# Attention on Trainium2: transposes and projections on 64x128 tiles, four double PSUM banks, loads by tensor, another order

## The chip, the core and the metric

The kernel runs on one NeuronCore of one Trainium2 chip. A core has five engines with queues of their own: PE (TensorE, matrix multiplies out of SBUF into PSUM), DVE (VectorE), ACT (ScalarE), POOL (GpSimd) and SP (SyncE, which here issues the transfers between HBM and SBUF). They meet only through semaphores. PSUM has eight banks. The metric is device time in microseconds (us) of one execution. Most executions of one kernel agree within 0.3%.

## What is computed

A linear attention over q, k, v of shape (8, 8, 576, 64) and then a mixture of eight experts on its result. The attention, per batch and head:

```python
def phi(x):
    proj = np.einsum('bhsd,df->bhsf', x, w_phi)                     # 64 -> 128
    proj = proj - np.max(np.abs(proj), axis=-1, keepdims=True)
    return np.concatenate([np.exp(proj), np.exp(-proj)], axis=-1)   # 256 features
q_p, k_p = (phi(q), phi(k))
kv = np.einsum('bhsf,bhsd->bhfd', k_p, v)
z = np.sum(k_p, axis=2)
num = np.einsum('bhsf,bhfd->bhsd', q_p, kv)
den = np.einsum('bhsf,bhf->bhs', q_p, z)[..., None] + 1e-06
return num / den
```

The expert stage takes the 4608 rows of 512, forms logits with `w_gate`, assigns rows to experts greedily by logit (576 rows to each), and runs `relu(x @ w1[e]) @ w2[e]`. All arithmetic here is float32 or finer splits of it.

## The kernel before

**Units.** Attention works in 16 units: a pair of batches times a pair of heads. Per unit `load` (line 105) brings q, k and v as tiles `qi`, `ki`, `vi` of 128 partitions x 2 x 9 x 64; `ki` and `vi` come in four transfers each, `qi` in two.

**Steps of a unit**, by the names that the plan uses. `kt` (line 165): nine 128x128 transposes of k on PE in three groups, copied to SBUF by ACT as `kh`. `kg` (line 152): the projection by `w_phi`, in three blocks of 12 matmuls on 64x64 tiles of the array, into a double bank. DVE then takes the maximum (`km`, line 156) and subtracts it (`ks`, line 159, tile `kt`), ACT takes both exponentials (lines 177, 178, tile `kP`). `kv` (lines 189, 194): k features times v, on 128x64 tiles and a last piece on 64x64. POOL sums the features (`ad`, lines 201 to 205). `bd` (line 222) and `z` (line 234) bring the sums and the gate weights into `kz`. For q: `qt` (line 243), `qg` (line 152), `qm` and `qs` on DVE, then `T` (line 255), 18 more 128x128 transposes, and the exponentials on ACT (line 258, tile `qP`). Last `num` (line 279): the numerators, denominators and logits on 128x64 tiles, in four pieces a unit, and for each the division on DVE (lines 283 to 298).

**PSUM.** Two single banks S0, S1 (transposes of q and k, z, num, counts), two double banks D0, D1 (projections, bd, T) and two single banks for kv.

**Order.** No loop order is written out. `Plan` (line 17) gets every step with its engine, a duration, a due time, its dependencies and the buffers that it takes and frees, and lists the steps; the program is then issued in that list's order, so each engine runs its queue strictly in it. Due times come from the table `ATT`. The plan also places pieces of the expert stage's preparation (`init`: tables made by POOL and DVE, lines 360 to 424) into the attention.

**After attention** comes the routing of the first expert (DVE and PE in turns, from line 433 on), then the expert stage.

Of the kernel before, what the change touches and what calls it, by code (L numbers as in the profile page):

```python
# [17 lines left out]
class Plan:  # L18
# [3 lines left out]
    SEM=40.; dl=0.; wp=6.  # L22
# [5 lines left out]
    def order(self):  # L28
# [7 lines left out]
        while left:  # L36
            best=None; horizon={}
            cand={}
            for x in left:
# [9 lines left out]
                if not ok: continue  # L49
                for kind,n,u in x['slot']:  # L50
                    h=held.setdefault(kind,[0.]*n)
                    z=[t for t in h if t is not None]
                    if not z: ok=False; break
                    r=max(r,min(z)+self.SEM)
# [35 lines left out]
def attention(ctx, tc, nc, q, k, v, w_phi, w_gate, xs, L, C, xp, cfg={}, after=None, later=None, count=None, init=iter(())):  # L90
# [3 lines left out]
    d=dict(TI=21.,kt=-4.,kg=0.,kv=4.,bd=4.,z=5.,zc=6.,qt=6.,qg=10.,T=2.5,num=26.,stay=2.,ks=4.,qs=4.,ns=5.,ng=6,ld=60.,nqP=8,init=25.,pitch=1.)  # L94
# [7 lines left out]
    p=ps.tile([128,512],F32,name='S0',bufs=1)  # L102
    for _ in range(cfg.get('nwarm',7)): PE.matmul(p,w[:,0:128],w,start=True,stop=True)
    T={}
    HS=S*D
    def load(u,first=lambda: None):
        bp,hp=divmod(u,NP)
        qi=sb.tile([128,2,9,D],F32,name='qi',bufs=2); ki=sb.tile([128,2,9,D],F32,name='ki',bufs=2); vi=sb.tile([128,2,9,D],F32,name='vi',bufs=3)
        T['q',u],T['k',u],T['v',u]=qi,ki,vi
        def put(t,p,s0,s1,x,b,row):  # L110
# [23 lines left out]
    dv=lambda n,ps_=True: (150 if ps_ else 110)+1.03*n-95  # L134
    ac=lambda n,ps_=True: (170 if ps_ else 200)+.83*n-100
    QI=227.
    def unit(u):
        bp,hp=divmod(u,NP)
        t0=u*d['TI']
        def add(name,eng,dur,due,fn,deps=(),mode=None,slot=(),frees=(),lat=None,after=0.):  # L140
            P.add((name,u),eng,dur,t0+due,fn,[(x,u) for x in deps],
                  lat={'PE':170.,'DVE':95.,'ACT':100.,'POOL':30.,'SP':0.}[eng] if lat is None else lat,mode=mode,slot=slot,frees=frees,after=after)
        add('ld','SP',600. if u else 0.,-d['ld'],lambda x: load(u) if u else None,slot=(('qi',2,('qi',u)),('ki',2,('ki',u)),('vi',3,('vi',u))),lat=4500. if u else 0.)
        def slots(*l): return tuple((kd,n,(kd,u) if len(z)==0 else (kd,u)+tuple(z)) for kd,n,*z in l)
        ld0=('ld',)

        def project(x,X,src,i0,i1):
            p=X['p']=bank(X['b'],[128,2,512])(x)
            for i in range(i0,i1):
                for c in range(2):  # L150
                    for r in range(2):
                        PE.matmul(p[64*(c^r):64*(c^r)+64,r,128*(i-i0):128*(i-i0)+128],src[64*r:64*r+64,i,64*(c^r):64*(c^r)+64],C['w'][64*r:64*r+64,:],start=True,stop=True,skip_group_check=True)  # L152
# [8 lines left out]
        for g in range(3):  # L161
            def pe(x,g=g):
                if g==0: T['kh',u]=sb.tile([128,9,128],F32,name='kh',bufs=2)
                p=T['ktp',u,g]=bank(('S',u,'kt',g),[128,3,128])(x)
                for i in range(3): PE.transpose(p[:,i],ch(T['k',u],3*g+i),ident)  # L165
            def act(x,g=g): A.copy(T['kh',u][:,3*g:3*g+3],T['ktp',u,g])
            due=d['kt']+d['ks']*1.5*g
            add(('kt',g),'PE',327.,due,pe,ld0,'A',slots(('S',NS,'kt',g),*((('kh',2),) if g==0 else ())),(('ki',u),),after=(5500.,9000.,10000.)[g] if u==0 else 0.)
            add(('kh',g),'ACT',ac(384),due+.4,act,(('kt',g),),frees=(('S',u,'kt',g),))
        for g in range(3):  # L170
# [8 lines left out]
            add(('kg',g),'PE',3*QI,due,pe,[('kh',g)],'Q',slots(('D',ND_,'kg',g)),(('kh',u),),after=8000. if u==0 else 0.)  # L179
            add(('km',g),'DVE',dv(768),due+.8,lambda x,X=X: maxima(X,'km',3),(('kg',g),))  # L180
            add(('ks',g),'DVE',dv(768),due+1.4,lambda x,X=X: differ(X,'kt',3),(('km',g),),slot=slots(('ktt',3,g)),frees=(('D',u,'kg',g),))
            add(('ke',g),'ACT',2*ac(768,False),due+2.,act,(('ks',g),),slot=slots(('kP',2)) if g==0 else (),frees=(('ktt',u,g),))
        for g in range(2):
            def pe(x,g=g):
                kP=T['kP',u]; v_=T['v',u]
                if g==0: T['kvps',u]=[ps.tile([128,256],F32,name='kv%d'%i,bufs=1) for i in range(2)]
                for i,b in KV[g]:
                    a,s_=divmod(b,9); c=a^i
                    PE.matmul(T['kvps',u][i][64*c:64*c+64,:],v_[:,a,s_,:],kP[:,b,:],start=b in (0,5,9,14),stop=False,skip_group_check=True)  # L189
                if g==1:  # L190
# [19 lines left out]
        def kvt(x):  # L210
            kt=T['kvT',u]=sb.tile([128,2,256],F32,name='kvT',bufs=2)
            for i in range(2): A.copy(kt[:,i],T['kvps',u][i])
# [677 lines left out]
```

## Time and profile before

| | us |
|---|---|
| median of 3 runs (857.32 to 858.21) | 858.2 |
| the profiled execution | 857.9 |
| its span, first to last instruction | 856.1 |
| PE busy in the span | 803.4 |
| DVE busy | 570.2 |
| ACT busy | 370.0 |
| POOL busy | 262.1 |

The profile is one execution. A row of a timeline gives the start from the span's start, the length, engine, source line, operation, tiles (written <- read), shape and count; in brackets stands how long the engine had been idle ahead of it and what ended the wait. A float32 matmul shows as two records on PE, a transpose as one. The shape of a PE row begins with the tile of the array, rows*columns. Ends of matmuls are modelled, so prices on PE are best read from one block's start to the next. PEld are the loads of the stationary operand, which run beside the matmuls. A row of stretches gives, after start, end and length, the busy time of each engine with the number of its instructions, then the granted PE clock, the share of the DMA engines and GB/s.

### The profile page before, as it was taken

The page shows a single profiled execution, that of the slowest core. Times are in us where ns is not written, and L with a number is a line of the kernel's source. Part 1 is how long each engine was busy: PE and PEld are TensorE (multiplying, and loading weights), DVE is VectorE, ACT ScalarE, POOL GpSimd, SP SyncE. Part 2 cuts the span into 40 slices and gives each one's busy share as a digit, 9 for nine tenths or more (in the row PEclk, how much of TensorE's full clock was granted, in tenths as well). Part 3 has the DMA queues.
Part 4 walks back from the last instruction along what each step waited for, and adds up shares of the span by engine and source line. Part 5 has one row for each costly group of instructions (what it writes and reads, how often), then busy time and mean ns, then how long its engine had stood idle before and what let it go on. Part 6 is the DMA issues. An engine that isn't in the chain of part 4 may idle for free.

```text
span 856.1 us, 24776 instructions
## 1 busy us (share of the span) xinstructions
PE 803.4 (94%) x10508; PEld 685.8 (80%) x10508; DVE 570.2 (67%) x1534; ACT 370.0 (43%) x691; POOL 262.1 (31%) x300
## 2 busy tenths in 40 slices
PE   4879999999999999758999999999999999999995
PEld 2768887887788878658979879889889798898984
DVE  1787788778867887577858658668667577461410
ACT  1646665566566565413334324333333243251410
POOL 1654455555555555111040130310301202401001
PEclk9999999999999999958999999999999999999999
DMA  8424444454445421134143340532233225610301
GB/s 170 116 54 113 114 114 126 118 135 121 117 120 134 117 58 31 57 114 131 54 147 118 129 147 35 177 131 95 97 118 123 83 104 185 214 63 38 118 13 43
DMA packets 73534, 91.88 MB, mean 107 GB/s; under 512 B 5280, under 2 KB 56512, under 8 KB 73424
## 3 DMA queue, kind: packets, MB, share of 16 engines
q1 hardware_dynamic: 67328, 71.32, 29.3%
q0 software_dynamic: 6096, 18.98, 6.5%
q8 instruction: 83, 1.36, 0.7%
q14 instruction: 27, 0.22, 0.1%
HBM read 71.40 MB, written 18.87 MB: 105 GB/s over the span
## 4 chain that ended last, share of the span: by engine, by line
PE 69%; issue 16%; DVE 7%; POOL 4%; DMA 2%; ACT 1%; SPq 0%; POOLq 0%; DVEq 0%; ACTq 0%
PE h L763 19%; PE y L792 16%; PE S L279 7%; PE D L152 6%; PE kv L189 4%; PE D L255 3%; PE y L807 2%; PE S L165 2%; PE S L243 2%; PE h L739 2%; PE S L234 2%; DVE km L156 1%; PE rps L530 1%; POOL out_dram L821 1%; DVE kt L159 1%
## 5 line engine op out<-in xcount | busy, mean ns | idle before, releaser
L763 PE MATMUL h<-xh,w1h 128*128 128x272 f32 (+1 forms) x512 | 145.9, 305 | 0.7 <-ACT xh L740 0.7
L763 PE MATMUL h<-xh,w1l 128*128 128x304 f32 (+1 forms) x512 | 143.9, 301 | 0.0
L774 ACT ACTIVATE fh<-h 128x272 fp32r<-128x272 f32 (+1 forms) x128 | 49.2, 384 | 134.5 <-PE h L763 122.1
L821 POOL DMA_INDIRECT out_dram<-ysb,idx x40 | 40.5, 1012 | 207.0 <-ACT ysb L815 203.5
L792 PE MATMUL y<-w2h,fl 128*128 128x512 f32 x256 | 102.0, 398 | 0.0
L792 PE MATMUL y<-w2l,fh 128*128 128x512 f32 x256 | 101.9, 398 | 0.0
L792 PE MATMUL y<-w2h,fh 128*128 128x512 f32 x256 | 101.5, 396 | 0.0
L763 PEld LDWEIGHTS h<-xh,w1h 128*128 128x128 f32 x512 | 97.2, 190 | 2.5 <-issue 1.2
L763 PEld LDWEIGHTS h<-xh,w1l 128*128 128x128 f32 x512 | 97.4, 190 | 0.0
L734 POOL DMA_INDIRECT xg<-xs,idx x40 | 40.0, 1000 | 178.2 <-issue 141.5
L763 PE MATMUL h<-xl,w1h 128*128 128x272 f32 (+1 forms) x512 | 91.4, 298 | 0.0
L778 DVE SCALAR_TENSOR_TENSOR fl<-h,fh 128x272 fp32r<-128x272 f32 (+1 forms) x128 | 52.8, 419 | 55.6 <-ACT fh L774 41.9
L201 POOL TENSOR_TENSOR ks<-kP 128x512 f32<-128x512 f32 x32 | 40.9, 1277 | 157.1 <-issue 130.2
L279 PE MATMUL S<-kz,qP 128*64 128x73 f32 x2304 | 87.4, 230 | 1.0 <-ACT xp L296 1.0
L279 PEld LDWEIGHTS S<-kz,qP 128*64 128x64 f32 x2304 | 78.1, 137 | 11.0 <-issue 9.1
L202 POOL TENSOR_TENSOR ks<-ks,kP 128x512 f32<-128x512 f32 x64 | 81.5, 1273 | 4.9
L258 ACT ACTIVATE qP<-D 128x768 f32<-128x768 f32 x96 | 72.5, 808 | 9.1 <-PE D L255 5.6
L763 PEld LDWEIGHTS h<-xl,w1h 128*128 128x128 f32 x512 | 75.5, 188 | 0.0
L815 ACT COPY ysb<-y 128x512 f32<-128x512 f32 (+1 forms) x40 | 21.8, 544 | 104.4 <-PE y L792 72.3
L156 DVE TENSOR_REDUCE km<-D 128x6 f32<-128x768 f32 x48 | 45.7, 953 | 29.4 <-PE D L152 29.2
L189 PE MATMUL kv<-kP,vi 128*64 128x256 f32 x512 | 60.9, 379 | 0.0
L156 DVE TENSOR_REDUCE qm<-D 128x6 f32<-128x768 f32 x48 | 45.6, 950 | 20.0 <-PE D L152 19.8
(177 smaller groups left out, 1550.5 us busy)
## 6 DMA issues: line engine op xcount, KB each, us to landing
raww<-in_moe_w_dram SPq DMA_DIRECT2D x64, 512.0 KB, 5.5
qi<-in_q_dram SPq DMA_DIRECT2D x32, 288.0 KB, 4.6
xs<-xp SPq DMA_DIRECT2D x16, 576.0 KB, 3.8
ki<-in_k_dram SPq DMA_DIRECT2D x32, 160.0 KB, 3.8
vi<-in_v_dram SPq DMA_DIRECT2D x32, 160.0 KB, 5.2
ki<-in_k_dram SPq DMA_DIRECT2D x32, 128.0 KB, 3.7
vi<-in_v_dram SPq DMA_DIRECT2D x32, 128.0 KB, 5.0
xg<-xs,idx POOLq DMA_INDIRECT x40, 3.5
```

The costliest lines, as they stand in the source:

```text
L152: PE.matmul(p[64*(c^r):64*(c^r)+64,r,128*(i-i0):128*(i-i0)+128],src[64*r:64*r+64,i,64*(c^r):64*(c^r)+64],C['w'][64*r:64*r+64,:],start=True ...
L156: V.tensor_reduce(m[:,:,0:n],X['v'],axis=AX.X,op=OP.max,apply_absolute_value=True)
L189: PE.matmul(T['kvps',u][i][64*c:64*c+64,:],v_[:,a,s_,:],kP[:,b,:],start=b in (0,5,9,14),stop=False,skip_group_check=True)
L201: if i==0: G.tensor_add(ks[:,:,a],X(0),X(1))
L202: elif i<3: G.tensor_add(ks[:,:,a],ks[:,:,a],X(i+1))
L258: for fh in range(2): A.activation(qP[:,fh].rearrange('p (b i) f -> p b (i f)',b=2),X['T'][:,:,0:384],AF.Exp,scale=1.0-2*fh)
L279: PE.matmul(p[64*ab:64*ab+64,j-j0,:],T['qP',u,jj][:,fh,o,64*ab:64*ab+64],T['kz',u][:,ab,fh,a^ab,:],start=fh==0,stop=fh==1)
L763: PE.matmul(p,ws[:,k,o:o+128],xx[:,k,o1:o2],start=n==0,stop=n==11)
L774: A.activation(hh[:,f,o1:o1+m1],p[:,0:m1],AF.Relu)
L778: V.scalar_tensor_tensor(hl[:,f,o1:o1+m1],p[:,0:m1],0.0,hh[:,f,o1:o1+m1],op0=OP.max,op1=OP.subtract)
L792: PE.matmul(p,hx[:,f,o:o+128],ws[:,f%2,:],start=n==0,stop=n==23)
L821: st=G.indirect_dma_start(out=ov,out_offset=bass.IndirectOffsetOnAxis(ap=iv,axis=0),in_=yv,in_offset=None)
```

## The change

*Tiles.* A 128x128 transpose becomes a pair of transposes on 64x128 tiles (`turn`): one for partitions 0 to 63, one for 64 to 127, each into its own bank of a double bank. A projection block becomes six matmuls on 64x128 tiles instead of twelve on 64x64. kv, z and num stay on 128x64, bd and kv's last piece on 64x64. The transposes of q and k come in two groups (3 and 6 of the nine) instead of three, and ACT's copies with them.

*Banks.* All PSUM tiles of attention come from four double banks D0 to D3. num and its division come in two pieces a unit instead of four; the last unit's scaling is done by DVE and no longer by ACT.

*Loads* of k, q and v are steps of their own, each with its own due time and its own wait for a free buffer.

*Order.* `ATT` gets an `off` table with a due time for each step, and tables `o0` and `oL` for the first and the last unit; the plan's costs change (`swc`, `swA`, `swO`, `wp`, `QI`, `QT`, `dv`, `ac`). A step may now ask for several buffers of one kind.

```diff
@@ load
-    def load(u,first=lambda: None):
-        bp,hp=divmod(u,NP)
-        qi=sb.tile([128,2,9,D],F32,name='qi',bufs=2); ki=sb.tile([128,2,9,D],F32,name='ki',bufs=2); vi=sb.tile([128,2,9,D],F32,name='vi',bufs=3)
+    def load(u,n,first=lambda: None):
+        bp,hp=divmod(u,NP); b=2*bp
+        x=dict(q=q,k=k,v=v)[n]
+        t=T[n,u]=sb.tile([128,2,9,D],F32,name=n+'i',bufs=3 if n=='v' else 2)
...
-    P=Plan(d['stay']*1e3)
-    ND_,NS=2,2
-    def bank(u_,shape):
-        return lambda x: ps.tile(shape,F32,name='%s%d'%(u_[0],x['buf'][u_]),bufs=1)
+    P=Plan(d['stay']*1e3); P.swc,P.swA,P.swO,P.wp=90.,85.,35.,d['wp']
+    ND_=4
+    def bank(u_):
+        return lambda x: ps.tile([128,2,512],F32,name='D%d'%x['buf'][u_],bufs=1)
+    def turn(p,n,f):
+        for i in range(n):
+            for r in range(2): PE.transpose(p[:,r,64*i:64*i+64],f(i)[64*r:64*r+64,:],ident[64*r:64*r+64,64*r:64*r+64])
+    halves=lambda p,n: p[:,:,0:64*n].rearrange('p r (i t) -> p r i t',t=64)
+    rows=lambda t: t.rearrange('p i (r t) -> p r i t',r=2)
...
+    BK=((0,3),(3,9))
...
-    QI=227.
+    QI,QT=239.,61.
...
-        add('ld','SP',600. if u else 0.,-d['ld'],lambda x: load(u) if u else None,slot=(('qi',2,('qi',u)),('ki',2,('ki',u)),('vi',3,('vi',u))),lat=4500. if u else 0.)
+        for n,nb in (('k',2),('q',2),('v',3)):
+            def f(x,n=n): load(u,n,(lambda: C.update(weights(ctx,tc,nc,w_gate,C))) if u==0 and n=='k' else lambda: None)
+            add(('ld',n),'SP',2950.,-d['ld']+(0. if n=='k' else .1 if n=='q' else .2),f,slot=slots((n+'i',nb)),lat=2200. if u or n!='k' else 3400.)
...
             for i in range(i0,i1):
-                for c in range(2):
-                    for r in range(2):
-                        PE.matmul(p[64*(c^r):64*(c^r)+64,r,128*(i-i0):128*(i-i0)+128],src[64*r:64*r+64,i,64*(c^r):64*(c^r)+64],C['w'][64*r:64*r+64,:],start=True,stop=True,skip_group_check=True)
+                for r in range(2): PE.matmul(p[:,r,128*(i-i0):128*(i-i0)+128],src[64*r:64*r+64,i,:],C['w'][64*r:64*r+64,:],start=True,stop=True,skip_group_check=True)
...
-                p=X['T']=bank(('D',u,'T',g),[128,2,512])(x)
+                p=X['T']=bank(('D',u,'T',g))(x)
                 t=X['t'].rearrange('p i r f -> p (i r) f')
-                for i in range(6): PE.transpose(p[:,i//3,128*(i%3):128*(i%3)+128],t[:,i],ident)
+                turn(p,6,lambda i: t[:,i])
...
-                    if u==NU-1:
-                        for j in range(n): A.activation(x_[:,j0+j,64*a:64*a+64],p[:,j,0:64],AF.Copy,scale=rd[:,j,:])
-                    else:
-                        V.tensor_mul(x_[:,j0:j1,64*a:64*a+64],p[:,:n,0:64],rd[:,:n].to_broadcast([128,n,64]))
+                for c in range(2): V.tensor_mul(x_[:,5*c:9 if c else 5,64*a:64*a+64],v_[:,c,0:5-c,0:64],rd[:,c,0:5-c].to_broadcast([128,5-c,64]))
...
-ATT = {'TI': 20.56, 'kt': -4.44, 'kg': -1.69, 'kv': 7.48, 'bd': 4.17, 'z': 4.87, 'qt': -1.35, 'qg': 6.68, 'T': 12.67, 'num': 33.16, 'stay': 2.23, 'ks': 2.72, 'qs': 4.94, 'ns': 4.35, 'nqP': 6}
+ATT = {'TI': 21.607, 'kt': -4.44, 'kg': -1.69, 'kv': 7.48, 'bd': 4.17, 'z': 4.87, 'qt': -1.35, 'qg': 6.68, 'T': 12.67, 'num': 33.16, 'stay': 5.079, 'ks': 2.72, 'qs': 4.94, 'ns': 4.35, 'nqP': 6, 'wp': 2929.132, 'off': {('ld', 'k'): -72.48, ('ld', 'q'): -53.32, ('ld', 'v'): -55.81, ('kt', 0): -3.08,
...
```

What the new order does to the queues, at three places. Lines of the new program are a few higher: 130 are the transposes, 158 the projections, 229 bd, 242 z, 285 num.

PE at the start of attention, before; `ki_96` is the first unit's k, `ki_119` the second's:

```order
L165 MATMUL S0_132<-ident_69,ki_96 128x128 x3
L165 MATMUL S1_137<-ident_69,ki_119 128x128 x3
L152 MATMUL D0_143<-w_65,kh_131 64x128 x12
L165 MATMUL S0_158<-ident_69,ki_96 128x128 x3
L243 MATMUL S1_166<-ident_69,qi_95 128x128 x3
```

and in the changed program, where `ki_97` is the first unit's k and `ki_113` the second's:

```order
L130 MATMUL D0_119<-ident_69,ki_97 128x64 x6
L130 MATMUL D1_126<-ident_69,ki_97 128x64 x12
L158 MATMUL D2_141<-w_65,kh_118 128x128 x6
L130 MATMUL D3_149<-ident_69,qi_110 128x64 x6
L158 MATMUL D0_156<-w_65,kh_118 128x128 x6
L158 MATMUL D1_171<-w_65,kh_118 128x128 x6
L158 MATMUL D3_180<-w_65,qh_148 128x128 x6
L130 MATMUL D2_195<-ident_69,ki_113 128x64 x6
```

The second unit's k moved from the second block to behind four projections of the first unit.

PE in a unit in the middle, before (z, a projection, transposes of k, q and T, num, projections):

```order
L234 MATMUL S_2254<-one,ks 64x1 x16
L152 MATMUL D_2275<-w,kh 64x128 x12
L165 MATMUL S_2289<-ident,ki 128x128 x3
L243 MATMUL S_2295<-ident,qi 128x128 x3
L255 MATMUL D_2300<-ident,qtt 128x128 x6
L279 MATMUL S_2310<-kz,qP 64x73 x16
L152 MATMUL D_2330<-w,kh 64x128 x12
```

and changed:

```order
L285 MATMUL D_2893<-kz,qP 64x73 x36
L242 MATMUL D_2937<-one,ks 64x1 x16
L130 MATMUL D_2965<-ident,qi 128x64 x12
L158 MATMUL D_2978<-w,kh 128x128 x6
L158 MATMUL D_2992<-w,qh 128x128 x6
L130 MATMUL D_3001<-ident,qtt 128x64 x12
L285 MATMUL D_3017<-kz,qP 64x73 x36
```

num and z, both on 128x64 tiles, now stand side by side, and the transposes and projections that follow are all on 64x128.

SP's queue behind the first unit's k, before:

```order
L113 DMA qi_95<-in_q_dram 64x2x576 x2
L113 DMA vi_97<-in_v_dram 64x2x320
L113 DMA vi_97<-in_v_dram 64x2x256
L113 DMA vi_97<-in_v_dram 64x2x320
L113 DMA vi_97<-in_v_dram 64x2x256
L113 DMA ki_119<-in_k_dram 64x2x320
L113 DMA ki_119<-in_k_dram 64x2x256
```

and changed:

```order
L114 DMA qi_110<-in_q_dram 64x2x576 x2
L114 DMA ki_113<-in_k_dram 64x2x320
L114 DMA ki_113<-in_k_dram 64x2x256
L114 DMA ki_113<-in_k_dram 64x2x320
L114 DMA ki_113<-in_k_dram 64x2x256
L114 DMA vi_166<-in_v_dram 64x2x320
L114 DMA vi_166<-in_v_dram 64x2x256
```

The second unit's k moved ahead of the first unit's v.

More of the change, by code (lines that the diff above doesn't have):

```diff
@@ L18 @@
 class Plan:
[L22 removed]
+    SEM=40.; dl=0.; wp=6.; swc=95.; swA=100.; swO=50.
     def __init__(self,stay=0.): self.t=[]; self.by={}; self.stay=stay
@@ L49, in order @@
                 if not ok: continue
+                want={}
                 for kind,n,u in x['slot']:
[L51 to L54, printed above, removed]
+                    h=held.setdefault(kind,[0.]*n); i=want[kind]=want.get(kind,-1)+1
+                    z=sorted(t for t in h if t is not None)
+                    if i>=len(z): ok=False; break
+                    r=max(r,z[i]+self.SEM)
                 if not ok: continue
@@ L101, in attention, with put @@
     w=sb.tile([128,512],BF,name='warm',bufs=1); V.memset(w,0.0)
[L102 to L103 removed]
+    p=ps.tile([128,2,512],F32,name='D0',bufs=1)
+    for _ in range(cfg.get('nwarm',7)): PE.matmul(p[:,0],w[:,0:128],w,start=True,stop=True)
     T={}
     HS=S*D
[L106 to L110 removed]
+    def load(u,n,first=lambda: None):
+        bp,hp=divmod(u,NP); b=2*bp
+        x=dict(q=q,k=k,v=v)[n]
+        t=T[n,u]=sb.tile([128,2,9,D],F32,name=n+'i',bufs=3 if n=='v' else 2)
+        def put(p,s0,s1,b,row):
             n=s1-s0
@@ L185, in pe @@
                 kP=T['kP',u]; v_=T['v',u]
-                if g==0: T['kvps',u]=[ps.tile([128,256],F32,name='kv%d'%i,bufs=1) for i in range(2)]
+                if g==0: T['kvps',u]=bank(('D',u,'kv'))(x)
+                kv=T['kvps',u]
                 for i,b in KV[g]:
                     a,s_=divmod(b,9); c=a^i
-                    PE.matmul(T['kvps',u][i][64*c:64*c+64,:],v_[:,a,s_,:],kP[:,b,:],start=b in (0,5,9,14),stop=False,skip_group_check=True)
+                    PE.matmul(kv[64*c:64*c+64,i,0:256],v_[:,a,s_,:],kP[:,b,:],start=b in (0,5,9,14),stop=False,skip_group_check=True)
                 if g==1:
@@ L210, in kvt @@
         def kvt(x):
-            kt=T['kvT',u]=sb.tile([128,2,256],F32,name='kvT',bufs=2)
-            for i in range(2): A.copy(kt[:,i],T['kvps',u][i])
+            T['kvT',u]=sb.tile([128,2,256],F32,name='kvT',bufs=2)
+            A.copy(T['kvT',u],T['kvps',u][:,:,0:256])
         kend=d['kv']+4*d['ks']
-        add(('kvt',),'ACT',2*ac(256),kend+1.,kvt,[('kv',1)],frees=(('kv',u),))
+        add(('kvt',),'ACT',ac(512),kend+1.,kvt,[('kv',1)],frees=(('D',u,'kv'),))
         def bdp(x):
-            p=T['kfp',u]=bank(('D',u,'bd'),[128,2,512])(x)
+            p=T['kfp',u]=bank(('D',u,'bd'))(x)
             for i in range(2):
@@ new lines, in unit, with pe @@
+            h=2*hp+a
+            X={}
+            due=d['num']+d.get('ns',5.1)*2*a
+            def pe(x,a=a,X=X):
+                p=X['p']=bank(('D',u,'num',a))(x)
+                for j in range(9):
+                    jj,o=divmod(9*a+j,6); c,m=divmod(j,5); m*=73
+                    for fh in range(2):
+                        for ab in range(2):
+                            PE.matmul(p[64*ab:64*ab+64,c,m:m+73],T['qP',u,jj][:,fh,o,64*ab:64*ab+64],T['kz',u][:,ab,fh,a^ab,:],start=fh==0,stop=fh==1,skip_group_check=True)
```

154 lines of the change are left out of this document (72 added, 82 removed).

## The prediction

> **What bounds the kernel now.** I read the stretches by stage first, to see which engine is full where.
>
> ```profile
> core 0: us, PE busy (x) PEld busy (x) DVE busy (x) ACT busy (x) POOL busy (x), PEclk, DMA share, GB/s
> 0.00:17.30 17.30, 5.28 (x13) 1.83 (x13) 1.98 (x5) 1.76 (x2) 2.89 (x8) 1.00 0.85 182
> ...
> 40.00:60.00 20.00, 15.46 (x258) 12.40 (x255) 16.98 (x46) 9.41 (x16) 14.22 (x17) 0.91 0.27 61
> 60.70:326.70 266.00, 259.97 (x5599) 216.83 (x5595) 210.98 (x453) 165.65 (x274) 137.44 (x130) 1.00 0.44 112
> 356.10:856.10 500.00, 474.44 (x3626) 415.05 (x3626) 303.55 (x953) 161.08 (x340) 85.02 (x121) 0.97 0.32 107
> ```
>
> Attention fills the first 356 us. In the first 17.3 PE works 5.3, and between 40 and 60 it works 15.5 of 20. From 60.7 to 326.7 (13 units, from one bd block to the bd block 13 units later) PE is busy for 260 of 266 us: a unit takes 20.46 us and PE sets it. DVE has 211 us in there, 16.2 a unit, and would be next. The 500 us behind attention are the expert stage. Its instructions stand in the same order in both programs on every engine from the routing on, so it should only move as a block. Everything the change can do lies in the first 356 us: PE's steady work, the 17.3 us in which PE does almost nothing, the dip at 40 to 60, and the hand-over.
>
> **Prices on PE.** Inside a steady unit the timeline gives them from one block's start to the next.
>
> ```profile
> 199.78 0.82 PE L255 MATMUL D<-ident,qtt 128*128 128x128 f32 x6
> 200.44 0.49 PE L165 MATMUL S<-ident,ki 128*128 128x128 f32 x3
> ...
> 202.99 0.68 PE L222 MATMUL D<-bd,kvT 64*64 64x72 f32 x32
> 203.59 1.10 PE L234 MATMUL S<-one,ks 128*64 128x1 f32 x32
> 204.62 0.89 PE L152 MATMUL D<-w,kh 64*64 64x128 f32 x24
> ...
> 206.15 0.82 PE L255 MATMUL D<-ident,qtt 128*128 128x128 f32 x6
> 206.90 1.23 PE L279 MATMUL S<-kz,qP 128*64 128x73 f32 x32
> 208.06 0.89 PE L152 MATMUL D<-w,kh 64*64 64x128 f32 x24
> 208.77 0.83 PE L152 MATMUL D<-w,qh 64*64 64x128 f32 x24
> 209.53 1.49 PE L279 MATMUL S<-kz,qP 128*64 128x73 f32 x40
> ...
> 214.33 0.89 PE L152 MATMUL D<-w,qh 64*64 64x128 f32 x24
> 215.15 1.24 PE L279 MATMUL S<-kz,qP 128*64 128x73 f32 x32
> ```
>
> Six transposes followed by the same tile shape take 0.66 us (199.78 to 200.44): 110 ns each. Followed by another shape they take 0.75 (206.15): leaving costs 0.09. A projection block (24 records, two per matmul) takes 0.71 when it is entered from another shape (208.06), 0.76 when it is left for another shape (208.77) and 0.82 when both happen (214.33). So the block itself is 0.71 + 0.76 - 0.82 = 0.65, entering is 0.06, leaving 0.11. One change of tile shape costs about 0.15 to 0.17 us.
>
> **Transposes.** Counted in the program, 576 transposes of 128x128 become 576 pairs of 64x128 tiles. Each tile of a pair streams 64 columns instead of 128. Do the two halves run abreast? The projection row says that row halves do: four 64x64 tiles finish 24 records of 128 columns in 0.65 us, 27 ns a record, where the transposes take 110 ns for one 128-column stream over the whole array; 27 is a quarter of it, so all four tiles, and with them both row halves, run at once. The stream of a pair is then half of 110, 55 ns. The load of the stationary operand is the open price, since each half now has a 128-column load of its own. No row shows a 64x128 load. The bd block gives one end: 32 records from 202.99 to 203.59, less 0.11 for leaving, are 0.49 us or 15 ns a record, each with a 64-column load of 64 rows. Twice the columns is 31 ns, a pair 62. The z block (203.59 to 204.62, less entering and leaving: 0.87 us, 32 records) gives the other: 27 ns per 64-column load of 128 rows, so 55 for 128 columns and 110 for a pair, which is no gain. I take 62: bd's tiles have 64 rows, as the new ones have. 576 x (110 - 62) = **-27.6 us**; bounds -31.7 (stream alone) to 0.
>
> ```profile
> L279 PEld LDWEIGHTS S<-kz,qP 128*64 128x64 f32 x2088 | 71.0, 137 | 9.5 <-issue 8.8 <-ACT kh L166 0.5 <-DVE kt L375 0.2
> L255 PEld LDWEIGHTS D<-ident,qtt 128*128 128x128 f32 x270 | 31.3, 142 | 5.3 <-issue 4.7 <-PE S L234 0.6
> ```
>
> The groups by line say the same from another side: a load of 128 columns lasts 142 ns, of 64 columns 137. Five ns for 64 more columns is far from the 55 that z's price would ask. The Trainium skill, "TensorE: Matmul & The Clock Gate", LDWEIGHTS, speaks against the change: a load takes as long as its columns want, however few rows it has, at columns / 1.2 ns. By it halving the rows saves nothing, 128 columns are 107 ns, and by estimate a pair would cost 107 if the two loads overlap: the transposes would win 2 us, not 27.6. That rows do not count fits the doubling of loads that I assume; the price does not fit the two rows above. What it would make of the time is close to rival B, which goes by z's row.
>
> **Changes of shape.** Transposes and projections now share one shape, 64x128. Along the whole of attention PE changes shape 213 times in the old program and 147 in the new (13 and 9 a unit). 66 x 0.15 = **-9.9 us**. The new shape's own cost of changing is in no row; by leaving alone (0.09) it would be -5.9, by the dearest change (0.17) -11.2.
>
> **Projections.** 96 blocks, each with 12 records on two 64x128 tiles instead of 24 on four 64x64. The stream per pass is the same 128 columns, so 0.65 us stays; 12 loads at 31 ns (0.37) lie under it. With two tiles instead of four there is less to hide a load's tail. If half a 31-ns load shows at each of 4 records, a block gets 0.06 longer: +6 us. I take **+2**; bounds 0 to +6.
>
> **Start.** In the old order PE's second block is a transpose of the next unit's k, and everything queues behind it.
>
> ```profile
> 9.19 0.45 PE L165 MATMUL S<-ident,ki 128*128 128x128 f32 x1 [1.67 <-DMA ki<-in_k_dram]
> 9.68 0.48 ACT L166 COPY kh<-S 128x384 f32<-128x384 f32 x1 [7.63 <-PE S L165]
> ...
> 15.64 0.66 PE L165 MATMUL S<-ident,ki 128*128 128x128 f32 x2 [6.00 <-DMA ki<-in_k_dram]
> 17.34 1.56 PE L152 MATMUL D<-w,kh 64*64 64x128 f32 x24
> ```
>
> The first unit's k is all there at 9.19 and its copy done at 10.16, but the first projection starts at 17.34, behind the next unit's load. The new order does both transposes of unit 0 first, then its projection: about 10.3, 7 us earlier. SP now issues k, q of unit 0, then k of unit 1 ahead of both v. All of them are queued in one row of transfers, so unit 1's k comes earlier by one v and later blocks (q of unit 1) come last; PE meets them after four projections. Not all 7 us hold, since PE is thin until DVE's chain runs: **-6.5**, bounds -3 to -8. Cover gone, a late k of unit 1 would cost what its load is late, at most the 6.00 seen here.
>
> **The dip.** The tables built on POOL and DVE during attention hold DVE up, and PE with it.
>
> ```profile
> 46.35 1.36 DVE L362 CAST k<-k_f 128x288 bf16<-128x288 f32 x1 [0.93 <-POOL k_f L360]
> 49.79 1.51 PE L255 MATMUL D<-ident,qtt 128*128 128x128 f32 x6 [4.13 <-DVE kt L159]
> ```
>
> That work is the same in the new program and still stands in DVE's queue between softmax pieces. Four double banks in place of two let PE go on for two more blocks (0.66 to 0.82 each) before a late DVE stops it: **-1.4**, bounds +2 (the four banks now also serve transposes, kv, z and num) to -4.
>
> **Hand-over.** The last unit's scaling moves from ACT to DVE.
>
> ```profile
> 352.47 2.50 PE L279 MATMUL S<-kz,qP 128*64 128x73 f32 x72 [0.99 <-ACT xp L296]
> 356.01 0.23 DVE L433 TENSOR_REDUCE m<-L 128x9 f32<-128x72 f32 x1
> ...
> 358.70 0.15 DVE L541 SCALAR_TENSOR_TENSOR fl<-rps,n 32x8 bf16<-32x8 f32 x1 [0.95 <-PE rps L469]
> ```
>
> PE's 0.99 us wait for ACT goes. Two DVE multiplies now stand ahead of fl; DVE idles 0.95 there, so they are covered unless PE's first routing matmul takes their bank and waits (then +0.7). Net **-0.3**, bounds -1 to +0.7.
>
> **Costed at nothing.** ACT's copies of the transposes come in two pieces instead of three with the same columns, and kvT in one instead of two; POOL's sums only move. ACT has 166 of 266 us, POOL 137, so PE's work covers both; without the cover a copy of 768 columns (twice the 0.48 of 384) would stand on the path once a unit, 16 us in all, as in A below. Each load now waits on SP for its own buffer, and behind a waiting load stand the next loads and the writes of `xs`. Nobody reads `xs` before the experts. The transfers have room: 112 GB/s in the steady units become 126 with shorter ones, and the start moved 182.
>
> **Sum**, against this execution's 857.9 us (span 856.1, 1.8 around it; the runs' median is 858.2): -27.6 - 9.9 + 2 - 6.5 - 1.4 - 0.3 = -43.7, so 814.2. A unit would be 20.46 - (27.6 + 9.9 - 2)/16 = 18.2 us.
>
> **Rivals.** *A: DVE takes over.*
>
> ```profile
> DVE qm L156 <- PE D L152: 15.9, 10, 1.8
> DVE rd L283 <- PE S L279: 15.7, 23, 0.8
> DVE km L156 <- PE D L152: 12.6, 17, 1.8
> ...
> L284 DVE RECIPROCAL rd<-rd 128x4 f32<-128x4 f32 (+1 forms) x52 | 9.6, 184 | 1.8
> ```
>
> The edit takes two reciprocals (0.18 each) from a unit, so DVE has 15.9 us of 18.2. If its waits for PE stay as long as now (44.2 us over 13 units, 3.4 each), a unit is 19.3, and 16 units end 16 us later: 830. For it: PE's blocks get shorter, DVE's do not. Against: these waits exist because PE is late. The Trainium skill, "TensorEngine Tiling (Array Packing)", PSUM Bottleneck, has this rule: packing speeds TensorE, not the emptying of PSUM. The trace so far shows PE, not DVE, full.
>
> *B: a pair costs 110.* Loads bind, by z's price. The transposes win nothing: 814.2 + 27.6 = 842.
>
> *C, the other side: the two loads of a pair go one after the other, each as long as the densest full-width transposes allow, 110.* A pair is then 220, 576 x 110 = +63.4 above B: 905. It decides from where B's 842 plus 576 x (p - 110) passes 858: p = 138 ns. Against it: 15 ns a load in bd.
>
> *D: more than I count at the start and in the dip*, -8 and -4 with transposes at 55: 806 or a little less.
>
> **Chances.** Forecast 0.70, A 0.12, B 0.09, C 0.04, D 0.05. The predicted time is 814. The range 804 to 830 holds the forecast, D and about half of A. A measurement here can tell about 0.2% (1.7 us) from no change: faster 0.94, same 0.02, slower 0.04.
>
> **What would show it.** Twelve records of the new transposes should take 0.37 us from start to start (0.66 is B, 1.3 is C); a projection block 0.65 to 0.72; the distance between bd blocks 18.2 us on average. The first projection should start near 10.3. The routing's first reduce, now at 356.0, should come near 311 to 313, with 500 us behind it. PE waits for DVE of more than 1 us a unit would speak for A. I am wrong if the units stay near 20 us, or if the stretch behind attention changes by more than 2 us.

## The result and the profile after

The changed kernel takes 824.4 us (median of 4 runs, 824.0 to 824.9) against 858.2 (857.3 to 860.6): a ratio of 0.960, 95% interval 0.958 to 0.962. The forecast was 814, its range 804 to 830. The profiled execution has a span of 822.7 us.

The stretches by stage of the kernel before, cut at PE's bd blocks (start to the first, to the third, to the fifteenth, to the routing's first reduce, the rest); after start, end and length come PE, PEld, DVE, ACT and POOL busy, then the granted PE clock:

```profile
0.00:35.80 35.80, 21.85 (x254) 14.16 (x255) 15.10 (x19) 13.00 (x22) 11.79 (x16) 1.00 0.70 152
35.80:80.50 44.70, 39.65 (x818) 32.79 (x822) 35.25 (x87) 25.05 (x42) 27.82 (x34) 0.96 0.38 95
80.50:326.70 246.20, 240.17 (x5171) 200.36 (x5167) 196.58 (x425) 153.07 (x253) 126.91 (x120) 1.00 0.44 111
326.70:356.00 29.30, 27.29 (x655) 23.49 (x647) 19.65 (x54) 17.67 (x38) 10.54 (x10) 1.00 0.15 43
356.00:856.10 500.10, 474.44 (x3626) 415.05 (x3626) 303.64 (x953) 161.18 (x340) 85.02 (x121) 0.97 0.32 107
```

The same five stretches of the changed kernel:

```profile
0.00:29.75 29.75, 23.28 (x251) 17.60 (x252) 16.46 (x21) 14.36 (x21) 13.24 (x19) 0.83 0.98 201
29.75:66.70 36.95, 31.82 (x667) 26.42 (x665) 32.84 (x78) 22.36 (x33) 26.26 (x31) 1.00 0.38 103
66.70:294.80 228.10, 220.38 (x4737) 189.39 (x4735) 188.66 (x390) 150.90 (x217) 127.11 (x121) 0.99 0.42 119
294.80:322.00 27.20, 25.93 (x662) 23.17 (x660) 19.52 (x52) 14.79 (x21) 10.57 (x10) 1.00 0.16 48
322.00:822.70 500.70, 474.19 (x3626) 414.60 (x3626) 304.45 (x955) 160.69 (x336) 85.11 (x121) 0.96 0.32 107
```

| stretch | forecast | measured |
|---|---|---|
| to the first bd | -6.5 | -6.1 |
| to the third bd (two units and the dip) | -5.8 | -7.8 |
| twelve units | -26.6 | -18.1 |
| to the routing's first reduce (two units and the hand-over) | -4.7 | -2.1 |
| behind | 0 | +0.6 |

The forecast column is the prediction's sum with 2.22 us a unit. The expert stage moved as a block. What is missing lies in the twelve units: 8.5 of the 10 us; the other four rows together miss by 1.6.

A piece of PE's timeline of the changed kernel shows the prices and the new wait:

```profile
190.31 0.89 PE L158 MATMUL D<-w,qh 64*128 64x128 f32 x12
191.03 0.34 PE L130 MATMUL D<-ident,ki 64*128 64x64 f32 x6
...
194.55 0.35 PE L130 MATMUL D<-ident,qi 64*128 64x64 f32 x6
196.63 0.59 PE L130 MATMUL D<-ident,ki 64*128 64x64 f32 x12 [1.74 <-DVE qtt L165]
...
199.31 0.53 PE L130 MATMUL D<-ident,qtt 64*128 64x64 f32 x12
199.77 0.92 PE L285 MATMUL D<-kz,qP 128*64 128x73 f32 x22
```

Six pairs, left for another shape, take 0.46 us (199.31 to 199.77); less 0.09 for leaving, 0.37, as forecast. A projection between its own shape takes 0.72 (190.31 to 191.03) where 0.65 was the price of before. And PE, whose queue is in strict order, waits 1.74 us for DVE. Over the thirteen middle units these are PE's longest waits (what, total, times, longest), out of 7.7 us in all:

```profile
PE D L130 <- DVE qtt L165: 5.2, 3, 1.7
PE D L130 <- PE D L158: 1.3, 3, 0.8
```

What DVE does ahead of that wait:

```profile
190.28 0.85 DVE L448 TENSOR_TENSOR scb<-L,m 128x72 bf16<-128x72 f32 x1
191.05 0.16 DVE L449 TENSOR_TENSOR di<-s,s 128x9 int32<-128x9 int32 x1
191.13 0.16 DVE L450 TENSOR_TENSOR s<-s,m 128x9 int32<-128x9 int32 x1
191.21 1.31 DVE L452 TENSOR_TENSOR scb<-scb,e_f 128x72 bf16<-128x72 bf16 x1
...
192.52 1.53 DVE L455 TENSOR_SCALAR di<-s 128x9 int32<-128x9 int32 x5
...
194.63 0.94 DVE L162 TENSOR_REDUCE qm<-D 128x6 f32<-128x768 f32 x1
195.50 0.22 DVE L464 TENSOR_TENSOR OH<-scb,sm 128x72 bf16<-128x72 bf16 x1
195.63 0.94 DVE L165 TENSOR_TENSOR qtt<-D,qm 128x768 f32<-128x768 f32 x1
```

From 190.28 to 194.63 it prepares the routing (the maximum's one-hot rows and digits), and the softmax step qm, whose subtraction frees the bank that PE waits for, stands behind. Pieces of 9 to 72 columns last 0.16 us or up to 1.3. POOL meanwhile:

```profile
189.77 1.27 POOL L208 TENSOR_TENSOR ks<-kP 128x512 f32<-128x512 f32 x1
191.12 1.31 POOL L209 TENSOR_TENSOR ks<-ks,kP 128x512 f32<-128x512 f32 x1
```

DVE's long pieces end about when POOL's additions end (191.13 and 191.04; 192.52 and 192.43). The Trainium skill, "SBUF — State Buffer", on the two separate sides, says that VectorE and GpSimd share a pair of ports which one instruction holds until it ends; these rows agree, and the run with the pieces in POOL's pause tests it.

### The profile page after: what moved, and what is told of

Read it like the earlier page. It is cut to its first block, busy times and chain, and to the rows that moved or that the text cites. A ratio compares the mean times of both kernels' runs of the same rounds, so it can differ in the third digit from the quotient of the medians.

```text
span 822.7 us, 23414 instructions
## 1 busy us (share of the span) xinstructions
PE 775.6 (94%) x9932; PEld 671.2 (82%) x9932; DVE 561.9 (68%) x1494; ACT 363.1 (44%) x625; POOL 262.3 (32%) x300
## 4 chain that ended last, share of the span: by engine, by line
PE 43%; issue 16%; POOL 2%; DMA 0%; POOLq 0%; ACT 0%; ACTq 0%
PE h L767 20%; PE y L796 17%; PE y L811 2%; PE h L743 2%; PE rps L534 1%; POOL out_dram L825 1%; POOL xg L738 1%; DMA xg<-xs,idx 0%; PE rps L611 0%; POOLq L889 0%; PE rps L541 0%; POOL spacer L824 0%; PE rps L548 0%; ACT ysb L819 0%; ACT xh L744 0%
## 5 line engine op out<-in xcount | busy, mean ns | idle before, releaser
L285 PE MATMUL D<-kz,qP 128*64 128x73 f32 x2304 | 80.3, 228 | 2.6 <-DVE kt L165 2.6
L285 PEld LDWEIGHTS D<-kz,qP 128*64 128x64 f32 x2304 | 75.6, 136 | 5.2 <-DVE kt L165 2.7
L162 DVE TENSOR_REDUCE km<-D 128x6 f32<-128x768 f32 x48 | 45.8, 954 | 28.8 <-PE D L158 28.7
L196 PE MATMUL D<-kP,vi 128*64 128x256 f32 x512 | 61.6, 382 | 0.0
L796 PEld LDWEIGHTS y<-w2h,fh 128*128 128x128 f32 x256 | 48.2, 188 | 9.0
```

What stands on the lines that cost most here:

```text
L162: V.tensor_reduce(m[:,:,0:n],X['v'],axis=AX.X,op=OP.max,apply_absolute_value=True)
L196: PE.matmul(kv[64*c:64*c+64,i,0:256],v_[:,a,s_,:],kP[:,b,:],start=b in (0,5,9,14),stop=False,skip_group_check=True)
L285: PE.matmul(p[64*ab:64*ab+64,c,m:m+73],T['qP',u,jj][:,fh,o,64*ab:64*ab+64],T['kz',u][:,ab,fh,a^ab,:],start=fh==0,stop=fh==1,skip_group_che ...
L796: PE.matmul(p,hx[:,f,o:o+128],ws[:,f%2,:],start=n==0,stop=n==23)
```

## The experiments

Two theories at the start. **S**: the prices of the prediction hold except the projection's, and PE waits at places where DVE's work for the routing stands in a block. **Rivals**: the gain came with order and banks and not with the tiles; DVE has become the bound as a whole (A of the prediction).

### Which part of the change is worth what

*The changed kernel again*, for comparison:

> The changed kernel once more, beside the three below, for their comparison and for a second trace. Both theories: 824 us (824.0 to 824.9 seen). In its first trace the granted PE clock fell to 0.50 twice inside attention, each time for about 3.4 us behind a wait of PE (271.5 to 274.9 and 281.7 to 285.1). If these spells follow from the waits alone, they stand at the same places again; if they hang on where a wait falls in a fixed time raster, they stand elsewhere, with the same waits in place.

824.6 us (823.1 to 825.7). The waits stand at the same places, with 1.74 in place of 1.73 at 271.4. The clock does not. The first trace, in steps of 3.41 us:

```profile
268.05:271.46 3.41, 1.70 (x28) 1.18 (x26) 3.41 (x10) 1.06 (x2) 2.08 (x3) 1.00 0.00 0
271.46:274.88 3.42, 3.40 (x58) 3.03 (x58) 2.81 (x4) 0.80 (x1) 0.00 (x0) 0.50 0.00 0
...
278.29:281.70 3.41, 3.18 (x75) 2.95 (x71) 1.48 (x9) 2.50 (x4) 1.50 (x2) 1.00 0.02 5
281.70:285.12 3.42, 3.23 (x42) 3.12 (x44) 2.21 (x4) 1.06 (x2) 3.19 (x4) 0.50 0.58 175
```

and the second:

```profile
267.80:271.20 3.40, 1.85 (x28) 1.19 (x26) 3.40 (x9) 1.06 (x2) 2.23 (x3) 1.00 0.00 0
271.20:274.60 3.40, 3.21 (x82) 2.95 (x84) 3.26 (x5) 1.98 (x3) 0.00 (x0) 1.00 0.02 5
```

The second execution has the same wait and keeps its full clock. So the spells do not follow from the waits alone. In the first trace the two units with spells took 41.9 us (252.8 to 294.8), in the second 39.0: 2.9 us. The second execution as a whole is only 0.8 us shorter (span 821.9). Behind attention it took 503.0 us where the first took 500.7, with the same instructions but 34.1 us at half clock in place of 30.7 at the start of that stretch. So most of what it gained in attention was lost there.

*Full transposes back*:

```diff
-            for r in range(2): PE.transpose(p[:,r,64*i:64*i+64],f(i)[64*r:64*r+64,:],ident[64*r:64*r+64,64*r:64*r+64])
+            PE.transpose(p[:,i//3,128*(i%3):128*(i%3)+128],f(i),ident)
```

(ACT's copies read the matching layout.)

> The changed kernel with its 576 pairs of 64x128 transposes made 576 transposes of 128x128 again; order, banks, loads and the projections on 64x128 stay. Theory (a pair costs 61 ns where a full transpose costs 109, and a change of tile shape 0.15 us): +576 x 0.048 = +27.6, and 259 changes of shape in place of 147, +16.8; of the 44 some 2 are hidden in waits that PE has now: 866 us (862 to 869). Rival (the gain came with order, banks and start, and a pair is no cheaper than a full transpose): only the changes of shape are dearer, 841. Second rival (PE is no longer the bound, DVE is): much of the 44 hides, under 850.

*Projections on 64x64 back* (the loop of 12 matmuls of before):

```diff
-                for r in range(2): PE.matmul(p[:,r,...],src[64*r:64*r+64,i,:],C['w'][64*r:64*r+64,:],...)
+                for c in range(2):
+                    for r in range(2):
+                        PE.matmul(p[64*(c^r):64*(c^r)+64,r,...],src[64*r:64*r+64,i,64*(c^r):64*(c^r)+64],C['w'][64*r:64*r+64,:],...)
```

> The changed kernel with its 96 projection blocks on four 64x64 tiles again (12 matmuls a block in place of 6); order, banks, loads and pairs of transposes stay. Theory (a block costs 0.72 us on two 64x128 tiles and 0.65 on four 64x64): -96 x 0.07 = -6.5, and 216 changes of shape in place of 147, +10.3: 828 us (826 to 831). Rival (the block's price is the same on both, and what looks like 0.07 comes from what stands around it): +10.3 alone, 834.5. In the trace a block that follows and precedes its own shape, or the block less entering and leaving, should be 0.65 by the theory, 0.72 by the rival.

*Both back*, so that order, banks and loads alone are left:

> The changed kernel with both kinds of tiles as they were before: 128x128 transposes and 64x64 projections; what stays of the change is order, banks and loads. Theory: 824.4 + 27.6 (transposes) - 6.5 (projections) + 68 changes of shape more (215, about as many as before's 213), 10.2 = 855.7, less some 2 hidden in waits: 852 to 857, so that order, banks and loads alone are worth 2 to 6 us of the 34. Rival (order and banks carry the gain, the tiles are a detail): under 842.

Measured: 850.8 us (850.6 to 853.3) with full transposes, 824.6 (822.9 to 827.0) with 64x64 projections, 842.4 (841.3 to 843.4) with both. All three lie below the theory's figure, by 13 to 15 us where the transposes are full, and 3 where not. Full transposes came out between the two theories (866 and under 850), both old tiles at the edge of the rival (under 842). Four steady units of the kernel before, of the run with both, and of the run with full transposes:

```profile
141.50:223.56 82.06, 80.27 (x1730) 66.88 (x1725) 65.52 (x142) 51.03 (x85) 42.28 (x40) 1.00 0.47 118
```

```profile
129.90:210.00 80.10, 79.80 (x1729) 65.62 (x1724) 62.12 (x131) 49.92 (x73) 42.32 (x40) 1.00 0.43 121
```

```profile
131.30:214.20 82.90, 82.80 (x1436) 67.78 (x1433) 62.49 (x131) 50.23 (x73) 42.20 (x40) 1.00 0.42 118
```

and of the changed kernel:

```profile
123.00:197.85 74.85, 72.46 (x1579) 62.24 (x1577) 62.63 (x131) 50.26 (x73) 42.37 (x40) 1.00 0.45 126
```

With slower tiles PE is busy 79.80 of 80.10 us and 82.80 of 82.90: the waits for DVE are gone. With the fast ones it idles 2.39. That the waits go was not in the theory's sums: 0.52 to 0.58 us a unit, 8 to 9 of the 13 to 15 us by which they were too high. By kind, us a unit (all PE rows of four units, start to next start, divided by four; idle is where a row had ended before the next began):

| | before | both old tiles | full transposes | 64x64 projections | changed |
|---|---|---|---|---|---|
| 36 transposes | 4.47 | 4.88 | 4.85 | 3.15 | 2.69 |
| 6 projections | 4.67 | 4.58 | 5.08 | 4.66 | 4.65 |
| num | 4.98 | 4.67 | 4.67 | 4.67 | 4.67 |
| kv | 4.14 | 4.20 | 4.31 | 4.19 | 4.30 |
| bd, z, count | 1.80 | 1.63 | 1.79 | 1.66 | 1.79 |
| idle | 0.45 | 0.08 | 0.02 | 0.43 | 0.60 |
| unit | 20.51 | 20.04 | 20.72 | 18.76 | 18.71 |

Three things follow. (1) From the second to the fourth column only the transposes change, with as many changes of shape (215 and 216): 4.88 - 3.15 = 1.73 us for 36, 48 ns each, which is the forecast's price (PE's whole busy time, with small differences in the other rows, falls by 1.63: 45 ns). (2) From the second to the third only the projections change: PE's busy time goes up by 0.74. The 44 further changes of shape (2.75 a unit) are 0.36 of it at 0.13, so a block is dearer by some 0.06 us. In the run with 64x64 projections a block is 0.65 again. Against it the changed kernel's busy time is 0.22 lower (18.33 to 18.11), since the changes that it saves outweigh its dearer blocks, but PE idles 0.17 more: the equal times come in part from the waits. (3) PE's busy time falls from 19.96 (both old tiles) to 18.11, by 1.85, but idle rises from 0.08 to 0.60: 0.52 of it, 8.3 us over 16 units, is given back as waiting. And the order alone, with tiles as before, is worth 15.8 us (858.2 to 842.4), where I had expected 2 to 6. In the profiled executions 5.2 of it lie ahead of the first bd, 4.9 in the stretch to the third, 5.6 in the twelve units; there it is PE's idle time, 0.9 us in place of 6.0. PE's busy time is nearly as before (19.96 and 20.06 a unit): num in two pieces takes 0.31 less, but the transposes, beside other neighbours, 0.41 more.

### Why PE waits

*One DVE step more a unit*:

```diff
-            V.tensor_reduce(m[:,:,0:n],X['v'],axis=AX.X,op=OP.max,apply_absolute_value=True)
+            for _ in range(2 if X.get('twice') else 1): V.tensor_reduce(m[:,:,0:n],X['v'],axis=AX.X,op=OP.max,apply_absolute_value=True)
```

> The changed kernel with one more DVE step a unit: the last maximum over q's projection is taken twice (0.95 us, 16 times, 15.2 us of DVE in all); nothing else changes. Theory S (PE is full but for the places where DVE's pieces and tables come together): most of it hides in the 2.7 us that DVE has free in a unit, +2 to +6: 826 to 830. Rival A of the prediction (DVE has taken over as the bound): all of it shows, +13 to +15: 837 to 840. If PE alone were the bound: +0 to +1.

841.7 us, +17 on the changed kernel, though one of the five runs took 833.5 and the others 840.8 to 843.5; the profile is of the fastest, and its granted clock is 0.972 where the others have 0.955 to 0.961. Four of its units:

```profile
126.50:205.30 78.80, 75.27 (x1579) 64.21 (x1577) 66.65 (x135) 50.50 (x73) 42.24 (x40) 0.98 0.43 121
```

A unit is 19.70, 0.99 longer, for 0.95 us more on DVE, which is busy 66.65 of 78.80. PE's idle time grows by 0.28 a unit; the rest shows as longer PE rows, part of them at half clock (0.98 on the mean here), so the four units overstate it: ten of the twelve middle units, without the two that hold half-clock spells, are 0.77 longer on average than in the second trace of the changed kernel. Most of the step shows, though DVE has 12 us free in the four units. That is nearest to rival A, but no range was met: the median lies above A's 837 to 840, the profiled execution (+9) between S and A.

*One DVE step less*:

```diff
+                if g<2 or u==0: maxima(X,'qm',3)
+                else: X['m']=QX[u,1]['m']; X['v']=X['p'][:,:,0:384].rearrange('p r (i f) -> p r i f',f=128)
```

> The counterpart of the run with one more DVE step a unit: here DVE takes one step less. The third block of q's projection (from the second unit on) uses the maxima of the second block, so its own maximum is left out (0.95 us, 15 times); its output differs for that. PE's instructions and their order stay. Theory S (PE's busy time is 18.1 us a unit, and the other 0.6, with the half-clock spells that follow some of these waits, is DVE being late): 6 to 10 us less than the changed kernel, 814 to 818, units near 18.2 us. Rival (the waits of PE come from the way the four banks are passed on, not from how much DVE has to do): within 2 us of 824.

822.4 us (821.6 to 825.7): 2 us less, at the edge of the rival's range and far from mine. PE's waits over the middle units:

```profile
PE D L130 <- DVE qtt L165: 5.1, 3, 1.7
```

The three waits are there as before, and the twelve units take 227.5 us (228.1); what was gained lies ahead of them. The step taken out stands behind the one that PE waits for, the block of the routing ahead of it. So for these waits it is not how much DVE has to do, but what stands ahead of that one step. That a step more costs most of its length and a step less gains nothing there is seen; that it is because the added step lies on PE's chain through a bank is argued.

*The block cut and spread* (no order but DVE's, and the counts'):

```diff
     out=P.order()
+    for u in (3,7,11): later_count(u,move([(('pr',i),u) for i in range(12)],2))   # one piece behind every second DVE step
```

> The changed kernel with DVE's pieces of the expert stage's preparation (for the first three pairs of batches: the maximum of the logits, its digits, the one-hot rows) cut smaller and set one behind every second softmax or division step of DVE, over about two units, in place of one block behind a division; the count of each pair on PE comes a unit or so later. All else, PE's and ACT's order too, stays. Theory S (the 5.2 us that PE's transposes of k wait for DVE's qtt in the 13 middle units come from that block): these waits go, some of the small ones come: 818 to 821. Rival (four shared banks make PE wait for any late DVE step, wherever the pieces stand): PE's waits move and their sum stays, 823 to 826.

820.8 us (819.6 to 822.1), 3.6 to 3.8 less than the changed kernel (824.4 and 824.6). The waits for qtt are gone, as S said; small ones for z's column (1.6) came, and those for xp grew (1.7 in all, 1.2 in the changed kernel).

*The block in POOL's pause*: the same with whole pieces, one behind each DVE step from the third maximum of q on.

> The changed kernel with the same pieces, not cut, set one behind each DVE step in the stretch of the unit in which POOL adds nothing (in the changed kernel POOL is idle for about 10 us a unit, and pieces of 9 to 72 columns last 0.16 to 0.22 us there, while the same kind lasts 0.71 to 1.31 where a POOL addition runs and ends when it ends); the count on PE comes later. Theory S with contention: the pieces cost DVE some 3 us a pair in place of the 6.2 they cost between 188.1 and 195.7, and PE's waits for qtt go: 817 to 820, and the pieces last 0.15 to 0.25 us each, the five digits together under 0.6 (1.53 now). Rival (these lengths have nothing to do with POOL): the pieces last as long as now, and the gain is that of spreading alone, within 1 us of the run with the pieces cut and spread.

The pieces of this run (its lines are 38 higher), and POOL's next row:

```profile
125.01 0.22 DVE L486 TENSOR_TENSOR scb<-L,m 128x72 bf16<-128x72 f32 x1
...
125.70 0.22 DVE L490 TENSOR_TENSOR scb<-scb,e_f 128x72 bf16<-128x72 bf16 x1
...
125.92 0.45 DVE L493 TENSOR_SCALAR di<-s 128x9 int32<-128x9 int32 x5
```

```profile
126.83 1.27 POOL L208 TENSOR_TENSOR ks<-kP 128x512 f32<-128x512 f32 x1 [7.17 <-issue]
```

0.85, 1.31 and 1.53 us have become 0.22, 0.22 and 0.45: the length of these pieces is POOL's doing. But the time, 822.5 us (822.5 to 822.9), misses: 2 us gained where 4 to 7 were expected, and less than by spreading. Its trace shows other waits in their place. The count, moved with the pieces, still makes DVE wait for PE in the midst of its queue. In the changed kernel that is

```profile
280.15 0.15 DVE L477 TENSOR_TENSOR n<-n,D 32x8 f32<-32x8 f32 x1 [2.05 <-PE D L473]
```

and here PE waits 3.2 us for xp (2.1 and 1.1), the scalings of num, and 1.6 for z's column, and two half-clock spells (276.4 and 296.9) stand near. That these eat up the gain is argued; the run below that moves the count bears on it.

*The tables spread too*:

```diff
+    move([('init',i) for i in range(40)],3)   # one behind every third DVE step
```

> The run before this one, and the tables that DVE and POOL build between 34 and 59 us set one behind every third DVE step, so that they reach to about 95 us. PE idles some 5 us between 38 and 60 us in the changed kernel, waiting for DVE's kt (2.58 at 50.60) and a bank (2.21 at 41.19). Theory (that is DVE's block of tables): 3 to 4 us less than the pieces in the gap alone, 814 to 816. Rival (the dip is the program filling its pipeline, whatever the tables do): no difference to the run before beyond 1 us.

819.5 us (819.4 to 822.1), 3.1 less than without: the difference is as expected, the time is not, since the run before had missed its own. The stretch from the first to the third bd falls to 32.7 us (28.8 to 61.5); the next two units are longer by 2.2 together. PE idles 0.96 us in that stretch, where it is 5.13 in the changed kernel: that was DVE's block of tables.

*The start's loads*: the first unit's v issued ahead of the second unit's k.

> The changed kernel with one difference on SP: the first unit's v is loaded ahead of the second unit's k, as in the kernel before. Theory (of the earlier start only PE's order matters, and the loads come in time either way): PE meets the second unit's k at 14.95 now, and v's 576 KB at some 200 GB/s make it 2.9 us later, so PE stalls there, but DVE has its chain of the first unit to do meanwhile: +0.5 to +2, 825 to 826.5. Rival (the order of the loads carries the start): +3 to +5.

824.3 us (822.8 to 826.2): no difference, where I had expected +0.5 to +2. PE waits 0.97 for k there, and the first bd still starts at 29.2 (29.75 in the changed kernel). The earlier start is PE's order, not the loads'.

### A version that beats both

The pieces in POOL's pause, the tables spread, and the count done behind a z, in the free half of z's double bank, with its subtraction behind z's column:

```diff
@@ z
+            if u in CNT: count(CNT[u],p[0:32,1,0:8],3)    # nine matmuls behind z's
@@ zk
             V.tensor_copy(kz,p[:,0,0:8])
+            if u in CNT: count(CNT[u],p[0:32,1,0:8],4)    # n - counts
```

> A version meant to beat both kernels. DVE's pieces stand in POOL's pause as in the run with the pieces in the gap, the tables are built one behind every third DVE step, and the count of each pair of batches, which had a bank and a wait of its own (DVE waited 2.05 us for it), is done by PE right behind a z into the free half of z's double bank and read by DVE right behind z's column. Theory S: against the run with gap and spread tables (819.5) the waits behind the count go (3 us of PE's waits for xp, and a half-clock spell or two): 814 to 818. Rival (what is left are waits of another kind): 819 to 820.

> The run before this one with a piece behind every second DVE step in place of every one. Theory S with contention: the pieces reach past POOL's pause, so some last 0.7 to 1.3 us again, but each delays DVE alone: within 1 us of the run before, on either side. If only the spacing mattered, 1 to 2 us less; if only POOL's pause, 1 to 2 us more.

815.3 us (814.7 to 818.7), a ratio to the kernel before of 0.950, 95% interval 0.949 to 0.952, and 9 us below the changed kernel; with a piece behind every second step 818.0 (817.5 to 820.3). Four units of the first, from the sixth bd, and PE's longest waits:

```profile
118.10:191.40 73.30, 72.14 (x1579) 62.04 (x1577) 58.98 (x131) 50.12 (x73) 42.12 (x40) 1.00 0.47 132
```

```profile
PE D L130 <- PE D L158: 1.5, 4, 0.8
PE D L158 <- DVE xp L303: 1.3, 2, 0.8
```

A unit is 18.33 with 0.29 idle, DVE is busy 58.98 in place of 62.63. The profiled execution is the slowest of the five; attention ends 9.1 us earlier in it (312.9 against 322.0), and the stretch behind takes 504.0. In the second version waits for qtt (1.6) come back, and the pieces that reach past POOL's pause last 0.90 to 1.25 us again: they cost more, as S with contention said, though by more than its 1 us. Added one after the other, the three moves (pieces, tables, count) gave 2, 3 and 4 us: 824.4, 822.5, 819.5, 815.3.

## Why the prediction was right or wrong

**Transposes, -27.6: right.** A gain of 48 ns a pair was forecast, 45 to 48 measured (4.88 to 3.15 for 36), so B and C are out. The rule of the Trainium skill that spoke against it ("TensorE: Matmul & The Clock Gate", LDWEIGHTS: 107 ns a pair by estimate) does not set the price of these pairs: 61 ns (0.37 us for six), although the profile gives one load of theirs 141 ns on average, so by it more than two are under way at once.

**Changes of shape, -9.9: right.** From full transposes to pairs PE's busy time falls by 2.59; less the pairs' 1.73, 0.86 is left for 7 changes a unit, 0.12 each (0.14 with 1.63 for the pairs), where 0.15 was forecast: 66 changes are 8 to 9 us.

**Projections, +2: mis-sized.** The upper bound came: 0.06 to 0.07 us a block, +6 over 96, by the runs with full transposes. I argued that half a load might show and then took a third of that. Some 4 us.

**The unit, 18.2: the step that failed.** It is 18.7 without half-clock spells. PE's savings were subtracted from a unit as if its waits stayed, because DVE had 15.9 us to do in 18.2. A share of busy time does not say where the work stands. DVE's work for the routing stands in one block, ahead of a step that frees a bank, and the faster PE runs into it (5.2 of its 7.7 us of waits): 0.60 idle a unit in place of 0.45, and against the new order with old tiles 0.60 in place of 0.08. In the sum of the prediction it is 0.15 x 16 = 2.4 us; as seen from the tiles, 8.3 us of their 29.6 are lost there. Rival A named the engine and its price was near (+16 on the sum, +10 came), and half of its mechanism: A had DVE's waits for PE stay as long. Over 13 units those for projections (km and qm) did, 28.5 us before and 29.3 after, while those for num (rd) fell from 15.7 to 0.7. So DVE is not full, as the run with one step less shows too; each of the two engines waits for the other, and PE for DVE mainly at three places. The sign for A that I set, PE waiting for DVE for over 1 us a unit, did not come (0.4 to 0.5).

**Not in the sum: half-clock spells.** Two in the twelve units of the profiled execution, 2.9 us by comparison with the other trace. There the twelve units are short of the forecast by 5.5 only, and the stretch behind attention is 2.9 longer than before, more than the 2 us that I had set as a sign of being wrong: the same loss in another place.

Together 4 + 2.4 + 2.9 is 9.3 of the 10 us. The sum is looser than it looks: changes of shape gave 1 to 2 us less than forecast, and the order took 1.6 off PE's busy time (20.06 to 19.96 a unit), which no term had. PE's busy time as a whole fell by 1.95 a unit where 2.22 was forecast, 4.3 us over 16.

**Start, -6.5: right, but by other steps.** -6.1 at the first bd. The first projection started at 8.85, earlier than the 10.3 forecast:

```profile
7.98 0.65 PE L130 MATMUL D<-ident,ki 64*128 64x64 f32 x14 [2.21 <-DMA ki<-in_k_dram]
8.85 1.65 PE L158 MATMUL D<-w,kh 64*128 64x128 f32 x12 [0.23 <-ACT kh L172]
10.30 1.01 PE L130 MATMUL D<-ident,qi 64*128 64x64 f32 x6
...
17.26 0.59 PE L130 MATMUL D<-ident,qi 64*128 64x64 f32 x12 [1.69 <-DVE kt L165]
```

It then ran at half clock (1.45 us to the next block's start), and PE waited for DVE's chain.

**Dip, -1.4: wrong in its reason.** The stretch was 2 us better than forecast, but PE's idle time in it is 5.13 us as before (5.05): four banks did not carry PE over DVE's tables. 1.3 us of what shortened it is num (216 records in place of 256), which come back at the end. The kernel before also has a half-clock spell in this stretch, at 49.8, but that it cost anything is not shown: the second trace of the changed kernel has one there too, at 42.5, PE idles 3.54 in it, and the stretch is as long, 36.93. With both old tiles it is 39.8, 4.9 less than before, so most of the gain came with order and banks; no run parts the two.

**Hand-over and end: short by 2.6 us**, of which those 40 records of num are 1.3. PE's idle time there, up to its first row behind the reduce, stays 3.8 us in both; the last unit has no next one to fill it.

**What the two errors hid.** The total is off by 10 us, but its split is off by more. Order, banks and loads alone brought 16 us where the sum has 8 (start, dip and hand-over), the tiles 18 where it has 35.5. That 824 is within 10 us of the forecast is in part luck: what order, banks and loads brought beyond their terms made up for nearly half of what the tiles fell short.

## What to carry to other kernels

When the bounding engine gets faster, look in the trace for the places where another engine's side work stands in one block ahead of a step that frees a shared buffer: here they decided, and not the other engine's busy share. Side work of a few columns belongs where it neither stands ahead of such a step nor shares ports with a long instruction of another engine. A change of tile is to be priced with the changes of shape that it makes in that order: projections on 64x64 and on 64x128 came out equal here, the one with cheaper blocks, the other with fewer changes and more waiting.

## What the runs showed of the hardware

Pieces of 9 to 72 columns on DVE take 0.16 to 0.22 us alone and up to 1.31 while POOL adds; in POOL's pause 0.85, 1.31 and 1.53 us (five pieces) became 0.22, 0.22 and 0.45. The long ones of the changed kernel's three blocks end within 0.1 us of the end of an addition. Moving three such blocks, the tables and a count, with no work removed, gave 9 us.

Inside attention PE's clock falls to one half for 3.41 us, or twice that, at a time. The Trainium skill, "TensorE: Matmul & The Clock Gate", The HAM clock gate, has a free-running window of that length, and the idle state after at least one idle window. The length agrees with the traces. The condition, by the idle time that the profile shows, does not: a window in which PE idled 1.71 of 3.41 us was followed by half clock, and so was one in which it idled 0.23, while in the other trace one with 1.55 was not. The one with 0.23 held all of z and of the count, whose rows stream 1 and 8 columns: 1.60 us. From 62 to 310 us the fourteen traces, each cut by its own steps of 3.41 us, have 1001 windows and 14 half-clock spells. All 14 follow one of the 23 windows in which PE's idle time and the rows of z and the count make 1.65 us or more together; none follows one of the other 978. So rows of a few columns seem to count as idle, and about half a window seems to be enough. No run tested this, and 9 of the 23 were not followed: what exactly counts as idle stays open. The two spells of the first trace cost 1.5 us each (2.9 together), and that the added DVE step gave runs from 833.5 to 843.5 us may come from such spells.
